# Five small clears on GpSimd behind each scatter of sorted rows

## The chip, the cores and the metric

The kernel runs on one core of a Trainium2 chip. The metric is the device time of one execution in microseconds (us). The engines of a core are TensorE (PE in the profile, with its weight loads as PEld), VectorE (DVE), ScalarE (ACT), GpSimd (POOL) and SyncE (SP); each runs its own list of instructions in order and waits for the others where it is told to. Transfers between the outer memory (HBM) and the core's memory are issued from SP's queue or, where rows are picked by an index, from GpSimd's.

## The reference

Attention over a window of 64 positions, then a layer of eight experts of which each token uses one, then a two-layer network.

```python
def _attn_ref(q, k, v):                      # 2 x 8 x 576 x 64
    scores = scale * np.matmul(q, k.transpose(0, 1, 3, 2))
    scores = np.where(mask, scores, -1e9)    # rel >= 0 and rel < 64
    attn = np.exp(scores - scores.max(-1, keepdims=True))
    attn = attn / (attn.sum(-1, keepdims=True) + 1e-09)
    return np.matmul(attn, v)
...
def _moe_ref(x, w_gate, w1, w2, capacity):   # x is 1152 x 512, 8 experts, 288 places each
    expert_idx = np.argmax(x @ w_gate, axis=1)
...
            disp[e, counts[e]] = x[i]        # rows sorted by expert, in order of the tokens
...
    h = np.maximum(np.einsum('ecd,edf->ecf', disp, w1), 0.0)
    y = np.einsum('ecf,efd->ecd', h, w2)
...
            out[i] = gate_w[i] * y[expert_idx[i], pos[i]]
...
def _moe2_ref(x, w_in, w_out, alpha):        # 512 -> 2048 -> 512
    h = x @ w_in
    g = np.maximum(h, 0.0) + alpha * np.minimum(h, 0.0)
    return g @ w_out
```

## The kernel before

The 1152 tokens are nine tiles of 128 rows. A loop over t = 0 to 10 works on three tiles at once in a fixed order: scores of tile t on PE (`sc`), masking and the row's peak on VectorE (`ms`), the exponential on ScalarE (`pt`); for tile t-1 PE turns the weights (`tp`, copied to `ptT`) and multiplies them by the values (`av`), which VectorE divides and puts into `xr`; for tile t-2 PE turns the columns (`tx`, copied to `xT`) and makes the eight gate logits (`lg`). The order of every engine's instructions is the order of the code (a manual schedule), and waits follow from the tiles that are read and written.

The tokens are routed in three batches: tiles 0 to 3 (`b0`), 4 to 6 (`b1`) and 7 and 8 (`b2`). For each batch VectorE finds every token's row in the sorted order (`sl`), and then `scatter` (L776) is called once a tile: GpSimd issues an indirect DMA (L777) that writes the tile's 128 rows of `xr`, 2112 bytes each, to their places in `xe` in HBM. The scatters of `b0` are issued while the loop is still at its last tiles; those of `b1` and `b2` come behind the loop, one after the other. `apart` (L210) declares that scatters don't depend on one another, as their rows are distinct, and has GpSimd clear one word (`spacer`, L215) behind each. Nine scatters are issued in all. At the end of the kernel nine indirect DMAs write the result to `out` (L1358) in the same way; they call `apart` as well, but not `scatter`.

The expert with most tokens is known after `b0`. For its first tokens PE picks the rows straight from `xr` with `pick` matrices (`pe_ahead`, the tile `xap`, copied to `axT` by ScalarE at L941) and runs both layers ahead with them (`go_ahead`: `aps`, `ah`, `atp`, `ay`). Behind the last scatter the gather `sx` (`star_rows`, L720) reads that expert's rows back from `xe`; it waits until all nine scatters have landed. SP's next weight loads (`raw`, L109) are held until it has landed ("rows first"), and PE turns its rows in `star_rest` (`atp<-identf,sx`). Then the other experts follow, whose rows are gathered with `rows_of` (L989, `xg`, and later the gates `gt`), and the two-layer network with its long runs of matmuls (`gps` and `ops`).

`xr` is one tile `[128, 9, 528]`; the pool `att`, in which it lies, has one buffer for each name and lasts as long as the attention.

Of the kernel before, what the change touches and what calls it, by code (L numbers as in the profile page):

```python
# [7 lines left out]
F32 = mybir.dt.float32  # L8
# [19 lines left out]
def attention_moe_mlp_kernel(  # L28
# [13 lines left out]
    nc = tc.nc  # L42
# [167 lines left out]
    def apart(earlier, ins):  # L210

        for x in earlier:
            tc.declare_no_dep(ins.ins, x.ins, reason="distinct rows")
        earlier.append(ins)
        nc.gpsimd.memset(spacer, 0.0)  # L215
# [6 lines left out]
    with tc.manual_schedule():  # L222
# [13 lines left out]
        with ExitStack() as es:  # L236
# [4 lines left out]
            att = es.enter_context(tc.tile_pool(name="att", bufs=1))  # L241
# [120 lines left out]
                           allow_small_or_imprecise_dtypes=True)  # L362
            nc.gpsimd.memset(xr[:, :, D:], 0.0)
            nc.gpsimd.tensor_copy(xr[:, :, D], tid)
            lane = att.tile([128, 2, NE], F32, name="lane")
            for h in range(2):
                nc.gpsimd.iota(lane[:, h], pattern=[[0, NE]], base=128 * h, channel_multiplier=1,
# [408 lines left out]
            def scatter(t, ts, sl):  # L776
                ins = nc.gpsimd.indirect_dma_start(  # L777
                    out=xe[:, :],
                    out_offset=bass.IndirectOffsetOnAxis(ap=sl[:, t - ts[0]:t - ts[0] + 1].bitcast(U32), axis=0),
                    in_=xr[:, t, :], in_offset=None)  # L780
                apart(scattered, ins)
                return ins

            def once(name, *shape, dtype=F32):
# [94 lines left out]
            def route(ts):  # L879
                yield from choosing(ts)  # L880
                yield from weighing(ts)
                while not pe_free:
                    yield
                pe_dispatch(ts)
                yield from dispatching(ts)
                sl = waiting[0][2]
                while waiting:
                    scatter(*waiting.pop(0))
                yield from choose_star()
                yield from count_star()  # L890
                yield from pick_star(ts, sl)

            for t in range(NTILE + 2):
# [15 lines left out]
                if t == NTILE + 1:  # L909
                    pe_ahead((0,))  # L910
                    dispatch(b1)
                    while waiting:
                        scatter(*waiting.pop(0))
# [37 lines left out]
            while waiting:  # L951
                scatter(*waiting.pop(0))
# [570 lines left out]
```

## Time and profile before

| | |
|---|---|
| three runs, median | 413.78 us (413.71 to 414.56) |
| the profiled execution, its own time | 415.7 us |
| its span, first to last instruction | 413.8 us |
| mean granted clock of TensorE | 0.980 |
| PE busy | 392.3 us, 95% |
| DVE, ACT, POOL busy | 284.9, 198.1, 56.5 us |

The profile is one execution. The 1.9 us by which its own time exceeds its span lie ahead of the first instruction and behind the last. In the rows below the first number of a timeline or of the chain is the start in us from the span's start, the second the duration in us; brackets hold the idle time of that engine just before, and what ended it. "remote", and "another core or an unknown queue" in the chain, is a wait for which the profile finds no instruction that ended at that time. The ends of PE's matmuls are modelled.

### The profile page before, as it was taken

The numbers are of one execution on the slowest core, as the hardware profiler recorded it, in microseconds if no ns is written. First come the engines' busy times: TensorE is split into PE (matmuls) and PEld (weight loads), VectorE is DVE, ScalarE is ACT, GpSimd is POOL, SyncE is SP. The second block draws the span as 40 slices with busy tenths as digits, with TensorE's granted clock in tenths as the row PEclk, the third lists the DMA queues.
The fourth block names the chain that finished last, engine by engine and source line by source line (L and its number), as shares of the span: only waits on it lengthen the run. The fifth ranks groups of instructions, "written<-read, shape, count | busy, mean of one in ns | idle before, by whom it ended". The sixth has DMA issues, their size and how long they took to land.

```text
span 413.8 us, 7875 instructions
## 1 busy us (share of the span) xinstructions
PE 392.3 (95%) x2931; PEld 348.6 (84%) x2932; DVE 284.9 (69%) x676; ACT 198.1 (48%) x371; POOL 56.5 (14%) x125
## 2 busy tenths in 40 slices
PE   7998769999999999999999999999999999999990
PEld 4887657789999998884999888998899988999880
DVE  4777674688997685457779966999829982356220
ACT  4877514566375444444467755675217720254000
POOL 5443055010007500000000000000000000000441
PEclk9999698999999999999999999999999999999997
DMA  7772966997898762796513334343401000000221
GB/s 251 227 202 68 339 260 204 407 373 268 280 295 286 234 209 106 268 328 218 203 54 102 117 138 151 108 143 108 153 0 55 0 2 0 0 2 1 79 101 56
DMA packets 20446, 66.12 MB, mean 160 GB/s; under 512 B 2992, under 2 KB 2992, under 8 KB 20400
## 3 DMA queue, kind: packets, MB, share of 16 engines
q1 hardware_dynamic: 17728, 57.74, 41.2%
q0 software_dynamic: 2528, 7.53, 5.2%
q8 instruction: 25, 0.41, 0.4%
q10 hardware_dynamic: 144, 0.26, 0.2%
q14 instruction: 21, 0.17, 0.2%
HBM read 60.74 MB, written 4.79 MB: 158 GB/s over the span
## 4 chain that ended last, share of the span: by engine, by line
PE 87%; DMA 4%; DVE 3%; another core or an unknown queue 2%; ACT 1%; issue 1%; SPq 1%; POOLq 0%; POOL 0%
PE gps L220 24%; PE ops L1350 24%; PE y L220 8%; PE hps L1049 7%; PE sps L220 4%; PE sy L220 4%; DMA v<-v_in 3%; PE aps L758 2%; PE pps L1217 2%; PE py L1232 2%; PE ay L769 2%; PE av L460 2%; DMA kT<-k_in 1%; PE tp L446 1%; PE xtp L1024 1%
## 5 line engine op out<-in xcount | busy, mean ns | idle before, releaser
L144 DVE TENSOR_TENSOR wlo<-raw,whi 128x1024 fp32r<-128x1024 f32 x45 | 54.2, 1225 | 18.4 <-ACT whi L1033 10.9
L220 PE MATMUL gps<-x2l,whi 128*128 128x384 f32 x192 | 64.3, 335 | 0.0
L220 PE MATMUL gps<-x2h,wlo 128*128 128x384 f32 x192 | 64.2, 335 | 0.0
L220 PE MATMUL gps<-x2h,whi 128*128 128x384 f32 x192 | 64.2, 335 | 0.0
L1350 PE MATMUL ops<-wlo,gh 128*128 128x512 f32 x144 | 56.1, 390 | 0.0
L1350 PE MATMUL ops<-whi,gl 128*128 128x512 f32 x144 | 56.1, 390 | 0.0
L1350 PE MATMUL ops<-whi,gh 128*128 128x512 f32 x144 | 56.0, 389 | 0.0
L1326 ACT ACTIVATE u<-gps,one 128x384 f32<-128x384 f32 x48 | 27.7, 577 | 58.9 <-PE gps L220 58.9
L1358 POOL DMA_INDIRECT out<-acc,tok x9 | 8.7, 965 | 255.0 <-ACTq L1392 242.2
L1356 DVE SCALAR_TENSOR_TENSOR acc<-ops,gate,acc 128x512 f32<-128x512 f32 x27 | 19.9, 747 | 33.1 <-PE ops L1350 33.1
L1327 DVE SCALAR_TENSOR_TENSOR g<-gps,slope,u 128x384 f32<-128x384 f32 x48 | 29.4, 613 | 19.0 <-ACT u L1326 18.9
L220 PEld LDWEIGHTS gps<-x2l,whi 128*128 128x128 f32 x192 | 36.1, 188 | 0.2
L220 PEld LDWEIGHTS gps<-x2h,whi 128*128 128x128 f32 x192 | 36.1, 188 | 0.1
L220 PEld LDWEIGHTS gps<-x2h,wlo 128*128 128x128 f32 x192 | 36.1, 188 | 0.0
L1033 ACT CAST whi<-raw 128x1024 fp32r<-128x1024 f32 x30 | 31.0, 1049 | 9.6 <-PE y L220 9.6
L1337 ACT ACTIVATE gh<-g,sign 128x384 fp32r<-128x384 f32 x48 | 29.3, 611 | 9.5 <-DVE g L1327 9.5
L1350 PEld LDWEIGHTS ops<-whi,gl 128*128 128x128 f32 x144 | 27.0, 188 | 5.7
L1350 PEld LDWEIGHTS ops<-whi,gh 128*128 128x128 f32 x144 | 27.0, 188 | 5.5
L1350 PEld LDWEIGHTS ops<-wlo,gh 128*128 128x128 f32 x144 | 27.0, 188 | 5.5
L1338 DVE SCALAR_TENSOR_TENSOR gl<-g,sign,gh 128x384 fp32r<-128x384 f32 x48 | 29.2, 608 | 0.2 <-ACT gh L1337 0.2
L190 DVE TENSOR_TENSOR wlo<-w,whi 128x512 fp32r<-128x512 f32 x32 | 22.0, 686 | 9.4 <-ACT whi L189 9.4
L220 PE MATMUL y<-hh,whi 128*128 128x256 f32 x96 | 27.6, 288 | 0.0
(273 smaller groups left out, 808.6 us busy)
## 6 DMA issues: line engine op xcount, KB each, us to landing
raw<-moe_in SPq DMA_DIRECT2D x61, 512.0 KB
raw<-mlp_in SPq DMA_DIRECT2D x32, 512.0 KB
v<-v_in SPq DMA_DIRECT2D x8, 260.0 KB
sw<-moe_in SPq DMA_DIRECT2D x4, 512.0 KB
qT<-q_in SPq DMA_DIRECT2D x6, 256.0 KB
kT<-k_in SPq DMA_DIRECT2D x5, 256.0 KB
qT<-q_in SPq DMA_DIRECT2D x2, 384.0 KB
kT<-k_in SPq DMA_DIRECT2D x2, 384.0 KB
```

The costliest lines, as they stand in the source:

```text
L144: eng.tensor_tensor(lo, raws.pop(split[c]), hi.bitcast(F32), op=ALU.subtract)
L190: nc.vector.tensor_tensor(lo, w, hi.bitcast(F32), op=ALU.subtract)
L220: nc.tensor.matmul(ps, wa[i], xa[j], start=start and n == 0, stop=stop and n == 2)
L1033: (nc.vector.tensor_copy if c % 4 == 3 else nc.scalar.copy)(ring_tiles(c)[0], raws[split[c]])
L1049: nc.tensor.matmul(ps[:, f, :], (hi, lo)[i][:, kk, fs], xt[j][:, kk, :], start=n == kk == 0, stop=n == 2 and kk == 3)
L1326: nc.scalar.activation(out=u, in_=ps, func=AF.Copy, scale=one[:, ft:ft + 1])
L1327: nc.vector.scalar_tensor_tensor(g, ps, slope[:, ft:ft + 1], u, op0=ALU.mult, op1=ALU.max)
L1337: nc.scalar.activation(out=gh, in_=g, func=AF.Copy, scale=sg)
L1338: nc.vector.scalar_tensor_tensor(gl, g, sg, gh.bitcast(F32), op0=ALU.mult, op1=ALU.subtract)
L1350: nc.tensor.matmul(ps, a_[:, ts_], b_[:, f % 2, :], start=f == 0 and n == 0, stop=f == 3 and n == 2)
L1356: nc.vector.scalar_tensor_tensor(acc[:, tt, :], ps, sc, acc[:, tt, :], op0=ALU.mult, op1=ALU.add)
L1358: ins = nc.gpsimd.indirect_dma_start(out=out[:, :], out_offset=bass.IndirectOffsetOnAxis(ap=tok[:, tt:tt + 1].bitcast(U32), axis=0), in_=a ...
```

## The change

One row of 128 words, `between`, is added to the pool `att`, and behind every scatter of sorted rows (behind the clear of `spacer` in `apart`) GpSimd clears it five times. The nine scatters that write `out` are not touched.

```diff
             nc.gpsimd.memset(xr[:, :, D:], 0.0)
             nc.gpsimd.tensor_copy(xr[:, :, D], tid)
+            between = att.tile([1, 128], F32, name="between")
             lane = att.tile([128, 2, NE], F32, name="lane")
...
                     in_=xr[:, t, :], in_offset=None)
                 apart(scattered, ins)
+                for _ in range(5):
+                    nc.gpsimd.memset(between, 0.0)
                 return ins
```

## Rows read from the trace of the kernel before

**Rows 1.** The page's engine table: busy us, share of the span, instructions.

```profile
PE 392.3 (95%) x2931; PEld 348.6 (84%) x2932; DVE 284.9 (69%) x676; ACT 198.1 (48%) x371; POOL 56.5 (14%) x125
```

**Rows 2.** Busy time by stage, sum over the stages from 54 to 206 us.

```profile
sum 152.00, PE 147.94 PEld 129.17 DVE 110.64 ACT 75.13 POOL 27.25; mean PE 9.86 PEld 8.61 DVE 7.38 ACT 5.01 POOL 1.82
```

**Rows 3.** The chain that ended last, in order of time.

```profile
38.76 4.45 another core or an unknown queue
...
50.50 0.17 DVE r L466
...
57.30 3.99 another core or an unknown queue
...
205.94 25.09 PE gps L220 x144
```

**Rows 4.** Timeline of PE and ACT, 38 to 74 us.

```profile
38.17 1.09 PE L446 MATMUL tp<-identf,pt 128*128 128x128 f32 x8
43.20 1.07 ACT L452 COPY ptT<-tp 128x512 f32<-128x512 f32 x2 [4.44 <-remote]
57.35 1.16 PE L702 MATMUL xap<-pick,xr 128*128 128x128 f32 x8 [0.98 <-issue]
61.31 0.37 ACT L941 COPY axT<-xap 128x256 f32<-128x256 f32 x1 [4.01 <-remote]
73.88 0.60 PE L732 MATMUL atp<-identf,sx 128*128 128x128 f32 x4
```

**Rows 5.** Timeline of GpSimd, 37 to 63 us.

```profile
37.14 1.19 POOL L777 DMA_INDIRECT xe<-xr,sl  x1 [6.14 <-DVE most L646]
...
39.59 0.09 POOL L215 MEMSET spacer<- 1x1 f32 x1
39.90 0.96 POOL L777 DMA_INDIRECT xe<-xr,sl  x1 [0.22 <-issue]
...
41.16 0.96 POOL L777 DMA_INDIRECT xe<-xr,sl  x1 [0.21 <-issue]
...
54.12 0.96 POOL L777 DMA_INDIRECT xe<-xr,sl  x1 [11.91 <-DVE lgs L491]
...
59.18 0.96 POOL L777 DMA_INDIRECT xe<-xr,sl  x1 [0.22 <-issue]
...
62.69 0.99 POOL L720 DMA_INDIRECT sx<-xe,ixe  x1 [2.47 <-DMA xe<-xr,sl]
```

**Rows 6.** Timeline of GpSimd and ACT, 137 to 143 us.

```profile
137.80 1.43 POOL L989 DMA_INDIRECT gt<-xe,ixt  x1 [0.30 <-issue]
...
139.49 0.60 ACT L1057 ACTIVATE hh<-hps 128x512 fp32r<-128x512 f32 x1 [3.58 <-remote]
...
140.78 0.94 POOL L989 DMA_INDIRECT gt<-xe,ixt  x1 [0.30 <-issue]
...
142.58 0.60 ACT L1057 ACTIVATE hh<-hps 128x512 fp32r<-128x512 f32 x1 [1.55 <-remote]
```

**Rows 7.** Timeline of GpSimd, 7 to 13 us.

```profile
7.74 0.28 POOL L322 TENSOR_SCALAR_AFFINE_SELECT mf<-z 64x128 f32<-64x128 f32 x1
8.09 0.28 POOL L325 TENSOR_SCALAR_AFFINE_SELECT mf<-mf 64x128 f32<-64x128 f32 x1
...
11.22 0.21 POOL L363 MEMSET xr<- 128x144 f32 x1
...
12.15 0.33 POOL L379 MEMSET rev<- 128x1 f32 x8
```

**Rows 8.** One stage: length, busy of PE, PEld, DVE, ACT, POOL, clock, DMA, GB/s.

```profile
43.00:46.00 3.00, 2.17 (x40) 2.17 (x42) 1.89 (x18) 2.81 (x8) 0.00 (x0) 0.50 0.98 351
```

**Rows 9.** Timeline of SP, 30 to 72 us.

```profile
47.10 4.87 SPq L712 DMA_DIRECT2D sw<-moe_in  x4
66.16 5.55 SPq L109 DMA_DIRECT2D raw<-moe_in  x7
```

**Rows 10.** The tile `raw`, 30 to 100 us: ns least, median, most; first and last start.

```profile
L1033 DVE CAST whi<-raw x2: 683/683/683, 84.4 to 92.6; 128x1024 fp32r<-128x1024 f32 x2
```

## The prediction

> **What bounds the kernel now.** I read the engine table first: PE is busy 392.3 of the span's 413.8 us [rows 1]. So a GpSimd edit can only cost or give time where PE is not busy, and that is early: over 54 to 206 us PE works 147.94 of 152.00 us [rows 2], and from 205.94 us on the chain of waits is matmul behind matmul almost to the end [rows 3]. I therefore read that chain above all for the stretch in which rows are scattered, 37 to 62 us. The reader should see two pieces there that name no engine: 4.45 us from 38.76 and 3.99 us from 57.30. Both end on ScalarE reading something that PE wrote.
>
> What is PE doing? By its timeline the transposes `tp` end at 38.17+1.09 = 39.26 us, but their reader starts at 43.20; `xap` ends at 57.35+1.16 = 58.51, its reader starts at 61.31 [rows 4]. PE has finished, yet nobody learns of it for 3.9 and 2.8 us. (Ends on PE are modelled, so PE itself may have been late; for the sum it makes no difference.) I set GpSimd's timeline beside it [rows 5]. The first hold lies inside the run of four scatters, 37.14 to 41.16+0.96 = 42.12, and ends 1.1 us after that run. The second lies inside the run of five, 54.12 to 59.18+0.96 = 60.14, and ends 1.17 us after it. Two smaller holds stand in a run of gathers at 137 to 142 us: readers of `hps` start at 139.49 and 142.58, both put down to no engine, the latter 0.86 us after the last gather's end at 140.78+0.94 = 141.72 [rows 6]. The chain has no such piece where GpSimd is quiet. So my reading: while indirect DMAs follow one another on GpSimd, PE's completions reach the others late, and once it falls quiet they come through some 0.9 to 1.2 us later.
>
> Against this reading: several PE results inside the same gather run are read on time, so the hold is not certain each time.
>
> **The change, part by part.** It removes nothing and moves nothing; no DMA is added. It adds five clears behind each of nine scatters, 45 instructions on GpSimd, plus 512 bytes of memory.
>
> *Price of a clear.* The trace has no clear of 1x128 words. The nearest by words per partition is `xr`, 144 words, 0.21 us; the present one-word `spacer` is 0.09 [rows 5, 7]. The five write the same words, so I let each wait for the one before; an instruction that works on what the one before wrote starts 0.07 us behind its end (7.74+0.28 = 8.02, next at 8.09) [rows 7]. That is 5 x (0.20+0.07) = 1.35 us. From below: eight clears of different words take 0.33 us together, 0.04 each, so 5 x 0.04 = 0.2 us [rows 7]; and nothing at all, should they fit into the 0.31 us that already lies between one scatter's end and the next one's start (39.59, when the `spacer` begins, to 39.90). I take 1.35, because of the row nearest in words. The pace of scatters, now 41.16 - 39.90 = 1.26 us, becomes 2.6 us, and the quiet gap grows from 0.31 to 1.66 us.
>
> *On GpSimd's own queue* nothing but scatters is waiting in 37 to 60 us. The first run would end at 42.12 + 3 x 1.35 = 46.2, long before the next scatter at 54.12. The clears behind the last scatter of all stand ahead of the gather `sx` [rows 5], but that one now starts 62.69 - 60.14 = 2.55 us behind the scatter's end, waiting for the rows to land, which hides 1.35 us.
>
> *The first hold.* A gap of 1.66 us is longer than the 0.9 to 1.2 us after which the held readers started. So the first release would come 1.0 us behind the first scatter's end, at 37.14 + 1.19 + 1.0 = 39.3 rather than 43.2: 3.9 us back at that step. It isn't all kept: the following steps (values, transposes, values again) meet the second, third and fourth scatter and wait for their gaps. The bound from above is the last release: the fourth scatter ends at 46.2, so the step behind the second `av`, which now starts on VectorE at 50.50 in the chain, can come at 47.2, 3.3 us earlier. From below, one step that misses a gap by a little waits another 2.6 us, and 0.7 is left. PE's clock helps: it stood at 1.2 GHz (0.50) over 43 to 46 us after PE had waited for that reader [rows 8]; a shorter idle may keep 2.4 GHz. I take 2.5 us.
>
> *The second hold.* With 2.5 us gained, the five scatters start at 51.6 and every 2.6 us, ending at 52.6, 55.2, 57.8, 60.4 and 63.0. `xap` would end at 58.51 - 2.5 = 56.0, against a release at 55.2 + 1.0 = 56.2 and a next start at 56.8: a hold of 0.2 instead of 2.8 us. Missed, it waits until 58.8, again 2.8 us, and saves nothing. Ends 0 and 2.6; I take 1.5.
>
> *What becomes late.* The gather `sx` waits for the last scatter's rows. It starts 62.69 - 59.18 = 3.51 us behind that scatter's start, so at 51.6 + 4 x 2.6 + 3.5 = 65.5, 2.8 us later, and the weight loads that SP holds back for it go out at 66.16 + 2.8 = 69.0 [rows 9]. PE turns the gathered rows at 73.88 [rows 4], with 4.0 us gained at 69.9: hidden by 0.9 us. If the gain is larger, this becomes the limit: with g us won at the first hold the rows come at 66.16 + 5.4 - g, so the whole gain can't pass 73.88 - 66.16 - 5.4 + g = 2.3 + g, 4.8 us at 2.5 and 5.6 at 3.3. The first of those weights is split on VectorE from 84.4 on [rows 10]; at 80.4 it still has 11 us. Should this cover be gone, each us of `sx` is a us of PE.
>
> Sum: 2.5 + 1.5 = 4.0 us. The profiled execution took 415.7 us, its span 413.8 and 1.9 around it, so 411.7. The median of the runs shown, 413.78, lies 1.9 below the profiled one; I carry the 4.0 us over unchanged: **409.8 us**. The likeliest case's own range is 0.7 + 0 to 3.3 + 2.6 us, cut at 5.6 by the gather: 408.2 to 413.1 us.
>
> The Trainium skill speaks against this. "SBUF — State Buffer", section "Who interferes with whom", says that only VectorE and GpSimd share ports, and "PE and ACT never wait on anyone". By that rule the two holds of 3.9 and 2.8 us [rows 3, 4] aren't GpSimd's doing, spacing it out gives nothing, and the sum would be 0. The rows place all four holds in GpSimd's runs, so I follow the rows. The second rival below is what this rule would make of the time.
>
> **Rivals.**
> *The hold lasts as long as the run (slower).* If what holds PE back isn't released in gaps (none of the three 0.31 us gaps at 38 to 41 us released anything), stretching the run stretches the hold. First run: release 3 x 1.35 = 4.05 us later; second: 4 x 1.35 = 5.4 more; 9.45 in all, 423.2 us. At 0.2 us for all five clears it is 7 x 0.2 = 1.4 and 415.2 us. It decides wherever a gap is shorter than the release needs: under about 0.9 us between scatters, so also if the clears cost under 0.6 us. For it: the gap ahead of the scatter at 59.18 released nothing though `xap` was done at 58.51 [rows 4, 5]. Against it: one held reader of `hps` started at 139.49, right behind the gather that ends at 137.80+1.43 = 139.23, with more gathers to come [rows 6]; so the end of the whole run isn't needed.
> *The holds aren't the scatters' doing (no change).* PE's completions may be late for a reason that has nothing to do with GpSimd, such as the weight loads that SP starts in the same stretch. Then PE's path stays and only `sx` is later, by 4 x 1.35 = 5.4 us at most, against 73.88 - 66.16 = 7.7 us of cover: 413.8 us. For it: the gathers from 62.69 us on, at the same pace, leave no nameless piece in the chain. Against it: SP issues nothing between 47.10+4.87 = 51.97 and 66.16 us [rows 9], and the second hold is there.
>
> **How the numbers follow.** What can be told from no change is 0.2%, 0.8 us. Release in the gaps 0.55, of which 0.03 end within 0.8 us; the lengthened hold 0.28; not the scatters' doing 0.17, of which 0.02 lose over 0.8 us through the gather. Faster 0.52, same 0.18, slower 0.30. With the two cases of opposite sign at 0.83 the range must reach into the slower one: of the 0.28 about half lies under 419 to 420 us, so 420.0 leaves out some 0.13 above; 407.0, a good us under the likeliest case's own range for a clock that stays up, leaves out some 0.06 below.
>
> **What will show it.** Five clears of about 0.2 us behind each scatter, starts 2.6 us apart (under 1.6 proves my price wrong). The 4.45 us piece at 38.76 becomes 1 us or less, with several pieces under 1.5 us behind later scatters; the 3.99 us piece shrinks; `aps` gets its second half before 59 us rather than at 61.7; the clock over 43 to 50 us stays above 0.5. The prediction is wrong if both nameless pieces end about 1 us behind the last scatter of their run again, at 47 and 70 us, or if they stay where they are. It is half right if they shrink and PE then waits for the rows of `sx`.

## The result and the profile after

| | before | after |
|---|---|---|
| median | 414.17 us (413.71 to 414.71, 4 runs) | 408.23 us (407.59 to 408.95, 4 runs) |
| profiled execution, its own time | 415.7 us | 408.95 us |
| its span | 413.8 us | 407.2 us |
| mean granted clock | 0.980 | 0.993 |

The ratio is 0.9857, with a 95% interval of 0.9831 to 0.9882: 5.9 us, or 1.4%, faster. The forecast was 409.8 us. (The median before is now of four runs, the three that were shown and one more.)

The engine table of the page after, against [rows 1]: the same PE instructions are 2.6 us shorter (the mean granted clock rose from 0.980 to 0.993), and GpSimd has 45 instructions and 10.2 us more.

```profile
PE 389.7 (96%) x2931; PEld 345.8 (85%) x2932; DVE 284.8 (70%) x676; ACT 198.1 (49%) x371; POOL 66.7 (16%) x170
```

GpSimd's timeline after, 37 to 64 us, against [rows 5]:

```profile
37.40 1.19 POOL L778 DMA_INDIRECT xe<-xr,sl  x1 [7.54 <-DVE most L647]
...
38.67 1.21 POOL L784 MEMSET between<- 1x128 f32 x5
40.04 0.97 POOL L778 DMA_INDIRECT xe<-xr,sl  x1 [0.17 <-issue]
...
42.43 0.97 POOL L778 DMA_INDIRECT xe<-xr,sl  x1 [0.17 <-issue]
...
49.90 0.97 POOL L778 DMA_INDIRECT xe<-xr,sl  x1 [2.68 <-DVE lgs L492]
...
60.09 0.97 POOL L778 DMA_INDIRECT xe<-xr,sl  x1 [0.17 <-issue]
...
63.97 0.99 POOL L721 DMA_INDIRECT sx<-xe,ixe  x1 [1.67 <-DVE wlo L144]
```

The five clears take 1.21 us, the scatters start 42.43 - 40.04 = 2.39 us apart instead of 1.26, and between the end of one and the start of the next lie 42.43 - 41.01 = 1.42 us instead of 0.31. Yet the ninth scatter starts only 0.9 us later than before (60.09 against 59.18): the second run could begin 4.2 us sooner, as PE was sooner.

The timeline of ScalarE and PE after, against [rows 4]. The readers that stood with "remote" now start right behind PE:

```profile
38.43 1.09 PE L447 MATMUL tp<-identf,pt 128*128 128x128 f32 x8
39.13 1.07 ACT L453 COPY ptT<-tp 128x512 f32<-128x512 f32 x2
...
52.61 1.16 PE L703 MATMUL xap<-pick,xr 128*128 128x128 f32 x8 [0.46 <-issue]
53.81 0.37 ACT L944 COPY axT<-xap 128x256 f32<-128x256 f32 x1 [1.25 <-PE xap L703]
...
67.49 0.63 PE L733 MATMUL atp<-identf,sx 128*128 128x128 f32 x4 [2.50 <-DMA sx<-xe,ixe]
```

(`ptT` x2 merges two copies; the first starts while PE is at the second half of `tp`'s record.) The chain of waits after has no nameless piece between 30 and 66 us; its last rows there name the new limit:

```profile
46.27 0.18 DVE r L467
...
63.97 3.39 DMA sx<-xe,ixe
...
67.49 0.63 PE atp L733 x4
```

Stage by stage, the clock over 43 to 46 us is 1.00 where it was 0.50 [rows 8] (columns as there):

```profile
43.00:46.00 3.00, 2.51 (x50) 1.99 (x51) 2.32 (x11) 1.19 (x4) 2.60 (x9) 1.00 0.98 384
```

And SP's weight loads behind the gather [rows 9] go out 1.2 us later than before:

```profile
67.37 2.07 SPq L109 DMA_DIRECT2D raw<-moe_in  x3
```

Behind `xap` PE multiplies the picked rows by the first layer's weights (`aps`). Before, it stands still before most of that work and then does it slowly; after, it does all of it in one go:

```profile
61.73 6.27 PE L758 MATMUL aps<-raw,axT 128*128 128x256 f32 x20 [2.36 <-ACT axT L941]
```

```profile
53.61 5.34 PE L759 MATMUL aps<-raw,axT 128*128 128x256 f32 x24
```

So the account of the profiled pair is: VectorE's `r` is 50.50 - 46.27 = 4.23 us sooner and ScalarE's second `axT` 61.31 - 53.81 = 7.50 us. PE's next transposes (`atp` on `ah`) start at 58.79 where they started at 67.84, 9.05 us sooner: the 20 `aps` behind the hold had a granted clock of 0.81 over 61.3 to 64 us and 0.70 over 64 to 68, and after the change it is 1.00. PE then waits 2.50 us for the gathered rows, so its `atp` on them is 73.88 - 67.49 = 6.39 us sooner, and the span is 6.6 us shorter. About 9 us were won, and 9.05 - 6.39 = 2.7 us of them were lost again to the gather.

### The profile page after: what moved, and what is told of

The parts are those of the page before. It is cut to its first block, busy times and chain, and to the rows that moved or that the text cites. A ratio compares the mean times of both kernels' runs of the same rounds, so it can differ in the third digit from the quotient of the medians.

```text
span 407.2 us, 7922 instructions
## 1 busy us (share of the span) xinstructions
PE 389.7 (96%) x2931; PEld 345.8 (85%) x2932; DVE 284.8 (70%) x676; ACT 198.1 (49%) x371; POOL 66.7 (16%) x170
## 4 chain that ended last, share of the span: by engine, by line
PE 88%; DMA 5%; DVE 3%; ACT 1%; issue 1%; SPq 1%; POOLq 0%; POOL 0%
PE gps L220 25%; PE ops L1353 24%; PE y L220 9%; PE hps L1052 7%; PE sps L220 4%; PE sy L220 4%; DMA v<-v_in 3%; PE pps L1220 2%; PE py L1235 2%; PE aps L759 2%; PE av L461 1%; DMA kT<-k_in 1%; PE sc L419 1%; PE xap L703 1%; PE tp L447 1%
## 5 line engine op out<-in xcount | busy, mean ns | idle before, releaser
L1036 ACT CAST whi<-raw 128x1024 fp32r<-128x1024 f32 x30 | 31.0, 1049 | 10.8 <-PE y L220 9.7
L189 ACT CAST whi<-w 128x512 fp32r<-128x512 f32 x32 | 19.6, 611 | 17.0 <-DVE w L177 17.0
```

Source lines behind the costliest of these rows:

```text
L189: nc.scalar.copy(hi, w)
L1036: (nc.vector.tensor_copy if c % 4 == 3 else nc.scalar.copy)(ring_tiles(c)[0], raws[split[c]])
```

## The experiments

The theory: a reader learns late of what PE has finished while indirect DMAs follow one another closely on GpSimd, and a quiet gap lets it through. Rivals: the gain is of something else in the edit (the new row of memory, the other instruction stream); a longer run makes a longer hold; the weight loads that share the stage do it; the bytes of the rows do it. Every experiment ran beside runs of the kernel before on the same chip, and its ratio is against those; their medians are given where they matter, since they differ. Diffs are against the changed kernel unless the text says otherwise, and `...` marks what they leave out. Each trace is of one execution, whose own time need not be the median.

**The change once more.** No edit.

> The changed kernel once more, beside the three below on one chip. If its gain is of the two holds and not of one chip, the ratio comes out at 0.983 to 0.989 again, with scatters 2.4 us apart, no nameless piece in the chain between 30 and 66 us, and the gather sx landing near 67.4 us as the last thing that PE waits for.

Measured: 408.5 us, ratio 0.9861 [0.9826, 0.9897]; scatters 2.38 us apart, no nameless piece, `atp` on the gathered rows at 67.06 us after a wait of 2.58 for them. The gain repeats.

**The same clears elsewhere.** Twenty clears ahead of the first scatter, none behind any.

```diff
+            for _ in range(20):
+                nc.gpsimd.memset(between, 0.0)
...
-                for _ in range(5):
-                    nc.gpsimd.memset(between, 0.0)
```

> Nothing is cleared behind a scatter; the row of 128 words is still there, and 20 clears of it run on GpSimd between 31 and 37 us, before the first scatter. Theory (the quiet gap between scatters frees PE's results): the gap is 0.31 us again, both holds come back (pieces of about 4.4 and 4 us without an engine in the chain), 414.2 us, within 1 us of the kernel before. Rival (the row's place in memory, or a changed instruction stream on GpSimd, moved the holds away): 408 to 409 us without holds.

Measured: 412.81 us beside 412.45, ratio 1.0004 [0.9979, 1.0029]. The row of memory and the additional instructions win nothing. The scatters are 1.27 us apart again, and the stall is back in another form: PE's own timeline shows it starting late, with nothing named that it waited for.

```profile
37.63 1.21 PE L421 MATMUL sc<-kT,qT 64*64 64x128 f32 x21
39.08 0.33 PE L421 MATMUL sc<-kT,qT 64*64 64x128 f32 x2 [0.25 <-issue]
39.83 0.45 PE L421 MATMUL sc<-kT,qT 64*64 64x128 f32 x4 [0.42 <-issue]
40.58 0.46 PE L421 MATMUL sc<-kT,qT 64*64 64x128 f32 x5 [0.31 <-issue]
41.31 0.50 PE L449 MATMUL tp<-identf,pt 128*128 128x128 f32 x2 [0.27 <-issue]
42.74 1.44 PE L449 MATMUL tp<-identf,pt 128*128 128x128 f32 x6 [0.93 <-issue]
```

32 `sc` and 2 `tp` took 37.63 to 41.81 us, 4.2 us; after the change 32 `sc` take 1.10. The scatters here run from 37.02 to 42.01 us. So it isn't only that readers are told late: PE itself can be the one that is held. (In the second run a reader is late as well: `axT` starts 61.55 - 59.68 = 1.87 us behind the end of `xap`.)

**One run of scatters alone.** Five clears behind the first four scatters only, then behind the last five only.

```diff
-                for _ in range(5):
+                for _ in range(5 if ts == b0 else 0):
```

```diff
-                for _ in range(5):
+                for _ in range(0 if ts == b0 else 5):
```

> Five clears behind the four scatters of the first batch only. Theory (each run of scatters makes its own hold): the first hold goes, 4.2 us as measured in the changed kernel; in the second run the hold of 2.8 us stays, and the gather isn't late: 414.2 - 4.2 = 410.0 us. Rival (the second hold follows from the first, as PE is then behind its order): both gone, and without the late gather 406 us.

> Five clears behind the five scatters of the second and third batch only. Theory: the first hold stays (a piece of 4.4 us), the second goes (3.7 us won at the second half of aps), but the last scatter starts 4 x 1.13 = 4.5 us later, so PE waits for the gathered rows: needed at 73.9 - 3.7 = 70.2, there at 66.2 + 4.5 + some 0.5 = 71.2; 414.2 - 2.7 = 411.5 us. Rival (the second hold isn't of the scatters): no gain, and the gather's 5 us lie under the 7.7 us of cover: 414.2 us.

Measured: 408.63 us, ratio 0.9918 [0.9887, 0.995], and 413.52 us, ratio 1.0009 [0.9985, 1.0032] (before 412.45). With the first run spaced, the first hold is gone. I had expected the second to stay; in the profiled execution it is not there, although its scatters carry no clears. They fell apart by themselves, as the third batch wasn't ready: scatters at 49.80, 51.07 and 52.33, then 55.83. That this pause is the reason is likely, but not shown: among the three at the old pace the longest wait is 0.8 us. With the second run spaced alone, the first hold stays, the second is gone, and the gather is issued at 67.59 us and `atp` comes at 71.06. That is 2.8 us before [rows 4], in a profiled execution that took 413.8 us against 415.7. Not all of it lasts: PE had waited 2.45 us for the rows, the granted clock was 0.70 over 70 to 75 us, and the eight `ay` took 5.13 us in the chain where they took 3.44 before. The time is 1.1 us above the median of before, not 2.7 below as expected, and this group's runs of before vary from 410.4 to 415.06 us; what the second run's clears are worth by themselves is not settled.

**How much of a gap.** One clear behind each scatter; two behind each but the last of all; five behind every second scatter. In each the old loop line gives way to one of these, in this order:

```diff
-                for _ in range(5):
+                for _ in range(1):
+                for _ in range(2 if t < NTILE - 1 else 0):
+                for _ in range(5 if t % 2 else 0):
```

> One clear instead of five behind each scatter, 0.24 us by the trace of the changed kernel, so a gap of some 0.5 us instead of 0.31 before and 1.4 after. Theory as predicted (PE's results come through only 0.9 to 1.2 us after a scatter's end): both holds stay and are longer by 3 and 4 times 0.2 us, 415.6 us. Rival (any work between two scatters that is more than the one-word clear is enough): no holds, and the gather of the star rows is late by 1 us only instead of 5, so PE doesn't wait for it: 405.5 to 406.5 us.

> Two clears behind each scatter of both runs but the last of all, a gap of some 0.8 us. Theory (a gap of that size suffices, as it did for the second run): no hold over 1 us in either run, pace 1.6 us, gather not the limit: ratio 0.977 to 0.984, as with five and two. Rival (the first run needs the longer gap): the first hold is back with 2 to 4 us, ratio 0.986 to 0.993.

> Five clears behind every second scatter only (t = 1, 3, 5, 7). Theory (results pass at the first gap, so a hold lasts no longer than the two scatters that follow one another): readers wait 0.5 to 2 us instead of 3.9 and 2.8, the gather is 3 us sooner than with five throughout: ratio 0.980 to 0.988. Rival (a hold, once begun, ends only with the run): pieces of 2.5 us or more in both runs, ratio 0.992 to 1.003.

Measured: 411.42 us, ratio 0.9973 [0.9948, 0.9997]; 410.9 us, 0.9925 [0.9894, 0.9956]; 408.36 us, 0.9855 [0.9826, 0.9885] (before 412.45 beside the first, 414.35 beside the others). For the first run the traces give the gap from one scatter's end to the next one's start, and the longest wait there of a reader for a result that PE had finished (reader's start less the end of PE's record, or less the end of the reader's own work before, where that is later):

| behind each scatter | gap, us | longest wait, us | after the end of the last scatter before it |
|---|---|---|---|
| nothing (before) | 0.30 to 0.31 | 4.14 (`ms`; `ptT` 43.20 - 39.26 = 3.94) | 0.99 (1.08) |
| one clear | 0.40 to 0.44 | 42.96 - 39.11 = 3.85 | 0.65 |
| two clears | 0.65 to 0.69 | 44.04 - 41.26 = 2.78 | 0.34 |
| five behind every second | 0.31 and 1.39 | 43.90 - 42.20 = 1.70 | 0.66 |
| five | 1.42 to 1.61 | 0.78 | 0.29 |
| ten | 2.66 to 2.80 | 0.73 | 0.26 |

VectorE's `ms` is the held reader of before that waits longest:

```profile
43.11 0.29 DVE L431 CUSTOM_DVE_ANT_0 ms<-sc,mf 128x128 f32<-128x128 f32 x1 [4.14 <-remote]
```

The pairs show the release best. The timeline of GpSimd and VectorE with five clears behind every second scatter:

```profile
38.65 0.97 POOL L778 DMA_INDIRECT xe<-xr,sl  x1 [0.17 <-issue]
39.64 1.20 POOL L784 MEMSET between<- 1x128 f32 x5
...
40.31 0.29 DVE L432 CUSTOM_DVE_ANT_0 ms<-sc,mf 128x128 f32<-128x128 f32 x1 [1.33 <-PE tx L477]
...
42.28 0.96 POOL L778 DMA_INDIRECT xe<-xr,sl  x1 [0.22 <-issue]
43.27 1.20 POOL L784 MEMSET between<- 1x128 f32 x5
...
43.90 0.17 DVE L467 TENSOR_SCALAR r<-av 128x8 f32<-128x8 f32 x1 [1.81 <-PE lg L487]
```

Each of these readers starts 0.7 us behind the end of its pair (39.62 and 43.24). The first of them does so in a gap, with two more scatters of the run to come, so a hold can end in a gap of 1.4 us and needn't last as long as the run. The time came as expected, the gather didn't: it is issued at 62.97 us, 0.5 us before that of five throughout (63.48), not 3.

With two clears the rival came: the gap of 0.65 us let the steps at 39 to 40 us through and then failed once, for 2.78 us; in the second run of that kernel nothing was held. (Its runs go from 408.59 to 413.3 us, and the trace is of one of 408.77.) With one clear neither the expected 415.6 us nor the rival's 406 came. The first hold stayed and got no longer, at a pace of 1.36 instead of 1.26 us; in the second run the wait behind `xap` was 58.82 - 58.15 = 0.67 us where it had been 2.80. Nor is a gap always needed: in that kernel `ms` starts at 42.20 us, 0.11 us before the end of the fourth scatter, after 3.38 us of waiting. So no shortest gap that suffices can be read from these runs; 1.4 us behind every scatter left no wait over 0.8 us.

**More, and less where it is late.** Ten clears; then, as another kernel, five in the first run, two in the second and none behind the last scatter.

```diff
-                for _ in range(5):
+                for _ in range(10):
+                for _ in range(5 if ts == b0 else 2 if t < NTILE - 1 else 0):
```

> Ten clears behind each scatter. Theory (with five the gather sx is already the last thing that PE waits for): scatters 3.6 us apart, the first run ends 4 x 1.2 us later, which eats the pause of some 3.6 us in front of the second, and the gather issues 5 to 7 us later than with five; no hold, but PE stands idle 5 to 7 us longer in front of atp, so the whole gain is gone: ratio 0.998 to 1.006 against before. Rival (the gap alone counts and the gather has room): as with five, 0.983 to 0.989.

> Five clears behind each scatter of the first run, two behind each of the second but the last, which has none. Theory (a gap behind each scatter lets PE's results through, and the late gather is what now ends the gain): both holds stay away, sx issues 1.2 + 4 x 0.72 = 4.1 us sooner than with five throughout unless its own data are later, PE no longer waits for it, and up to 2.5 us more is won (the wait in front of atp with five throughout): ratio 0.978 to 0.984 against before. Rival (two clears, a gap of some 0.8 us, are too short for the second run): the second hold is back with 1 to 4 us, the gather early for nothing: ratio 0.986 to 0.993, as with the first run alone spaced.

Measured beside 414.85 us: ten 419.06 us, ratio 1.0102 [1.007, 1.0134], slower than before; five and two 406.53 us, 0.9805 [0.9774, 0.9835], the largest gain of all. PE's timeline with ten clears, and its stages (length; busy of PE, PEld, DVE, ACT, POOL; clock, DMA, GB/s):

```profile
74.66 1.08 PE L733 MATMUL atp<-identf,sx 128*128 128x128 f32 x4 [10.21 <-DMA sx<-xe,ixe]
```

```profile
70.00:75.00 5.00, 0.34 (x2) 0.38 (x3) 0.00 (x0) 0.00 (x0) 3.18 (x5) 0.50 0.33 88
75.00:80.00 5.00, 5.00 (x10) 2.40 (x9) 3.30 (x7) 2.48 (x3) 1.89 (x2) 0.50 0.83 256
```

No hold there, but PE stands 10.2 us for the gathered rows, 7.6 us more than with five (67.06 to 74.66), and then works at 1.2 GHz: in the chain the eight `ay` take 5.71 us, where they took 3.44 with five clears. The span is 10.8 us longer than with five. The later `atp` is 7.6 of them; the clock makes `atp` 0.45 us and the eight `ay` 5.71 - 3.44 = 2.3 us longer, most of the other 3.2. I had expected the first part and not the second. With five and two, PE's timeline:

```profile
62.42 1.88 PE L770 MATMUL ay<-sw,axT 128*128 128x512 f32 x4
64.23 0.63 PE L733 MATMUL atp<-identf,sx 128*128 128x128 f32 x4
```

PE goes from `ay` to the gathered rows without a pause, since the gather was issued at 59.70 instead of 63.48 us. Beside the changed kernel on the same chip this is 408.5 - 406.5 = 2.0 us, within the 2.58 us of waiting that are gone. (The two intervals touch by 0.0009.) Two clears throughout keep a hold in the first run and win less.

**What in a scatter does it.** Three kernels built on the one before, without clears. In the first each scatter writes only the last 16 words of a row (64 of 2112 bytes), so that the rows' features are left out (nine early transfers fill them with zeros, and `s8` holds the places of the 64-byte pieces); in the second the first `raw` load waits for the first run's last scatter; the third is the first with reads in place of the writes (token numbers are laid down beforehand, gates are left out too).

```diff
+            for j in range(NTILE):
+                nc.sync.dma_start(xe[128 * j:128 * j + 128, :D], ahead_y)
...
+                nc.vector.tensor_scalar(s8[ts], sl, ROW / 16, D / 16, op0=ALU.mult, op1=ALU.add)
...
-                    out=xe[:, :],
...
+                    out=xe.rearrange("n (c e) -> (n c) e", e=16),
...
-                    in_=xr[:, t, :], in_offset=None)
...
+                    in_=xr[:, t, D:ROW], in_offset=None)
```

```diff
-                    paced(load(c), 3)
+                    paced(load(c, scattered[-1] if c == 0 else None), 3)
```

```diff
-                    out=xe.rearrange("n (c e) -> (n c) e", e=16),
...
-                    in_=xr[:, t, D:ROW], in_offset=None)
+                    out=read[:, t, :], out_offset=None,
+                    in_=xe.rearrange("n (c e) -> (n c) e", e=16),
...
```

> The kernel before, no clears; each scatter writes only the last 16 words of its 128 rows (the rows' 512 features are left out and stay zero), so it makes as many descriptors, one after the other as before, for a thirty-third of the bytes. If the descriptors that GpSimd makes hold PE's results back: scatters again 1.26 us apart, both nameless pieces in the chain as before (near 3.9 and 2.8 us), time within 0.5% of before. If it is the rows' transfer: the holds go without any gap, and with the gather not later the time is 405.5 to 408 us where before is 413.8 (ratio 0.980 to 0.986).

> The kernel before, no clears; the first raw load waits for the last scatter of the first run (one more dependency), so while those four scatters are issued no weights are in flight. If back-to-back scatters alone hold PE's results: the first nameless piece stays at 3 to 5 us, and with the loads some 5 us later the time is 412 to 417 us (ratio 0.995 to 1.008). Rival (scatters hold only together with the weight loads that share the DMA engines): the first hold is under 1 us, PE's results are taken at once at 39 us, and the time is 408 to 411 us (0.984 to 0.992).

> As the narrow scatters (no clears, 64 bytes for each of 128 rows, the 512 features left out and zero), but each of the nine indirect DMAs reads its 128 pieces from the rows' memory into SBUF instead of writing them there (tokens are laid down in row order beforehand, gates are left out). Same number of descriptors, same bytes, same place, other direction. If any back-to-back indirect DMAs hold PE's results in this stage: a nameless piece of 3 to 5 us in the first run, as with the narrow scatters (4.90 us). If only writes do: no piece over 1 us there, and the time 3 to 5 us under that of the narrow scatters (ratio to before 0.978 to 0.988).

Measured: narrow 411.74 us beside 414.85, ratio 0.9923 [0.9897, 0.9949]; late loads 414.37 beside 414.35, 0.9997 [0.9973, 1.0021]; reads 405.16 beside 405.58, 0.9999 [0.9984, 1.0013]. The chain of waits with narrow scatters (they start at 40.21 us here and end at 45.19), and then the chain, the stage and SP's timeline with late loads:

```profile
41.15 4.90 another core or an unknown queue
```

```profile
38.31 4.41 another core or an unknown queue
```

```profile
40.00:43.00 3.00, 0.00 (x0) 0.00 (x0) 0.38 (x3) 0.29 (x1) 1.53 (x4) 0.98 0.60 232
```

```profile
43.60 3.53 SPq L109 DMA_DIRECT2D raw<-moe_in  x4
```

With a thirty-third of the bytes the first hold is no shorter: VectorE's `r` starts at 46.07 us where `av` ended at 41.18, 4.89 us. So it isn't the number of bytes. I had expected both holds and a time within 0.5%; the second run fell into 3 and 2 scatters here and held less (waits of 1.30 and 0.61 us), and the narrow kernel's 0.8% goes the same way. With no weight load issued until 43.60 us the first hold is there all the same (42.71 - 38.82 = 3.89 us), and all 0.70 MB that moved over 40 to 43 us were those of the scatters; so it isn't the loads either. What is left is the 128 pieces of an indirect DMA, their making on GpSimd or their handling behind it; no run here tells these apart.

The reads decided nothing, for a reason worth more than the answer. They ran on another chip, and there **the kernel before took 405.58 us** (9 runs, 404.66 to 406.3), less than any version elsewhere. The trace of the reads has no nameless piece, but it shows that this isn't their doing: much later, where this kernel issues its gathers 1.25 us apart just as the one before does, the readers of `hps` aren't held either. ScalarE's rows there:

```profile
126.63 0.60 ACT L1066 ACTIVATE hh<-hps 128x512 fp32r<-128x512 f32 x1 [1.29 <-PE hps L1058]
129.93 0.60 ACT L1066 ACTIVATE hh<-hps 128x512 fp32r<-128x512 f32 x1 [1.75 <-PE hps L1058]
```

They start 0.03 and 0.04 us behind the end of the last `hps` that each reads (126.60 and 129.89). On the other chips the same two readers are late in the kernel before ("remote", [rows 6]) and in the changed one, whose gathers have no clears. ScalarE after the change:

```profile
133.15 0.60 ACT L1060 ACTIVATE hh<-hps 128x512 fp32r<-128x512 f32 x1 [3.58 <-remote]
...
136.21 0.60 ACT L1060 ACTIVATE hh<-hps 128x512 fp32r<-128x512 f32 x1 [1.52 <-remote]
```

In all 13 other traces, of 12 kernels, these two readers are 1.25 to 3.09 us late, in some of them under the name of PE instead of "remote". So this chip doesn't hold what the others hold, as far as one trace shows. No trace of the kernel before was taken there; that its 405.58 us come from scatters that hold nothing is likely and not shown. If so, spacing them has nothing to win there; whether five clears cost something there wasn't tried.

## Why the prediction was right, point by point

*The mechanism* stood as put: holds inside the two runs of scatters, gone when the scatters are spaced. The same clears elsewhere gave nothing, the first hold came without weight loads and with few bytes, and readers passed in a pair's gap. Both rivals fall: the hold did not stretch with the run, and it is the scatters' doing. The 0.9 to 1.2 us that a release was taken to need were too long, though: with pairs it came after 0.7 us, with five clears after 0.3, and with one and two clears some results passed although the gaps were 0.40 to 0.69 us. By the rule of the Trainium skill ("SBUF — State Buffer", section "Who interferes with whom") that PE and ScalarE never wait on anyone, spacing would have given 0, as the prediction read it; 5.9 us came. The rule stands there among the SBUF's ports, and whether the hold has to do with ports, no run here shows.

*The price of a clear* was 1.35 us for five and measured 1.21; the pace 2.6 and measured 2.39 us.

*The first hold* is the term that was most mis-sized: 2.5 us taken, 3.3 the bound, 4.23 measured. The first step came as put, at 39.13 us where the working had 39.3, but with some luck: nothing was released there, as ScalarE had only just finished its own work and PE the first half of `tp`. What failed was "the following steps ... meet the second, third and fourth scatter and wait for their gaps". Mostly they don't: with 1.4 us between scatters PE's results pass while one is being issued, too (`tx` ends at 39.96, and ScalarE copies it to `xT` at 40.09, within the scatter of 40.04 to 41.01). The one step that looks as the text had it is `r` at 46.27, after the longest wait left, 0.78 us: it starts 0.29 us behind the fourth scatter, which ended at 45.98. The bound had 1.0 us behind 46.2. The step gained even more than the hold of 3.94 us; the clock, named but not priced, stayed at 2.4 GHz over 43 to 46 us.

*The second hold* gave 7.50 - 4.23 = 3.27 us, taken 1.5, bound 2.6. It is the hold of 2.80 whole, and 0.5 more in front of `xap` (0.98 us of "issue" before, 0.46 after).

*The clock behind the second hold* had no term in the sum, and it gave 9.05 - 7.50 = 1.55 us more: the `aps` that follow that hold ran in part at 1.2 GHz before, 20 of them in 6.27 us, and at 2.4 GHz after, 24 in 5.34.

*The gather* was right and decided the end. I wrote that the whole gain can't pass 2.3 + g: with g = 4.23 that is 6.5, and `atp` came 6.39 us sooner. Part of that closeness is luck: the fifth scatter of the run started 10.19 us behind the first, 5.13 more than before and not 5.4, and the gather 3.88 us behind it instead of 3.51. At my g of 2.5 the gather was "hidden by 0.9 us"; with all that PE had gained it waited 2.5 us for it, the half-right case that the text named. The five-and-two version takes that back.

So two terms were too small and one was missing, and a cap that was right cut what they gave: 4.0 us forecast, 5.9 measured.

*The small holds in the gather run* were read as the same thing; that both are missing on the third chip together with the holds fits it, and no run spaced those gathers. They cost little, as PE has other work there. Over the 20 us that contain them before, by stage:

```profile
125.00:145.00 20.00, 19.82 (x157) 19.10 (x157) 14.94 (x17) 10.68 (x15) 13.42 (x11) 1.00 0.79 259
```

## What to carry to other kernels

Where the chain names no engine, set the timelines of the others beside the gap: a reader that starts late behind a finished matmul, mostly 0.3 to 1.2 us behind the end of a row of indirect DMAs, is a stall that a few cheap instructions between them can remove. Space them only until the hold goes, and least where something waits for the last one: here five, then two, then none (406.5 us) beat five throughout (408.5) and ten (419.1). And follow the gain past the hold: what PE does next may get a higher clock, and what comes later by the spacing may become the new limit. Compare on one chip, and run the kernel before there as well: a gain of this kind can be there on one chip and have nothing to work on in another.

## What was not expected of the hardware

- Chips of the same kind differ in whether back-to-back indirect DMAs hold PE's results: the two readers of `hps` are 1.25 to 3.09 us late in 13 traces and 0.03 and 0.04 us in the one of the third chip. The kernel before takes 412.45 to 414.85 us (medians beside the experiments) on two chips and 405.58 on the third.
- The hold can show as PE itself starting late in bursts of 2 to 6 matmuls, with 0.25 to 0.93 us of "issue" between them, rather than as readers that are late.
- Fewer bytes don't shorten it: with 64 bytes for each of 128 rows the first hold was 4.89 us, with 2112 bytes 4.14.
- After 10.2 us without matmuls PE ran at 1.2 GHz until about 80 us, and the eight `ay` took 5.71 us instead of 3.44: an idle wait can cost more than itself. The length of the wait alone doesn't tell: after 2.45 us (second run spaced alone) they took 5.13, after 2.50 us (five throughout) 3.44.
